# Experts of a routed MoE: a short last tile in 16 instead of 24 matmuls, and a first product with four widths

## The chip, the cores and the metric

The kernel runs on one core of one Trainium2 chip. The metric is the time of one execution in microseconds (us) on the device. TensorE (PE, its weight loads PEld) multiplies, VectorE (DVE), ScalarE (ACT) and GpSimd (POOL) work on tiles of 128 partitions, and SyncE (SP) issues most transfers. Each engine has a queue of its own and runs it in order.

## The reference

Three stages follow each other: a block-recurrent attention over 2 x 768 tokens, a dense layer pair with squared ReLU, and a routed layer with eight experts. The change touches the last one:

```python
for e in range(E):                       # E = 8, N = 1536 tokens, D = 512, F = 1024
    mask = e_idx == e                    # e_idx = argmax(x @ w_gate)
    h = np.maximum(x[mask] @ w1[e], 0.0)
    ye = h @ w2[e]
    out[mask] = gate_w[mask, None] * eom[mask, e, None] * ye
```

On the reference's own inputs the eight experts get 180, 334, 245, 166, 121, 47, 176 and 267 tokens.

## The kernel before

**Numbers in two parts.** Every float32 operand of a large product is split into a high part and a rest (`hh` and `hl`, `xh` and `xl`, `w1h` and `w1l`), both in a reduced format (fp32r). A product is three matmuls: high by high, high by rest, rest by high.

**Tiles of an expert.** The tokens of an expert are numbered and gathered into up to three tiles of 128 rows (`NG` = 3; expert 0 has `NSL` = 2). An expert's 1024 hidden columns are eight blocks f of 128. `emm1(e, f)` is the first product of a block: 12 matmuls whose moving operand is the tokens, so their columns are the tokens. A branch on TensorE takes 384, 256 or 192 columns by the expert's count `cnt[e]`; expert 0 always takes 256. Its result, in one of two PSUM buffers, becomes `hh` on ScalarE (L914) and `hl` on VectorE (L915), so the first product of block f waits for `hl` of block f - 2.

**The second product.** `emm2(e, f, j)` adds block f of tile j into the accumulator `ea[j]`: three matmuls of 128 weight columns and 512 moving columns, `hh` by `w2h`, `hh` by `w2l`, `hl` by `w2h`. Tile 0 is done between the first products, two blocks behind. Tile 1 follows in one piece if the count is over 128 and tile 2 if it is over 256 (branches at L1031 and L1035); otherwise TensorE jumps over them.

**The end of an expert.** `put(e, j)` scales tile j by its gate on ScalarE (L926, output `y`) and GpSimd scatters the rows to the output (L927). The puts are issued for every tile, whether TensorE had it or not; rows without a token are left out by the scatter's index. ScalarE's queue then comes to `hh` of the next expert's block 0.

**Side work.** The weights of the experts are loaded and split between the blocks (L776 on ScalarE, L777 on VectorE). In expert 0 the routing of the last 512 tokens is finished on VectorE between the blocks (`route_count`, `slot_idx`, `route_gate`, `route_gates`), by a table `late` of jobs for each block. The order on each engine is that of the program text.

Of the kernel before, what the change touches and what calls it, by code (L numbers as in the profile page):

```python
# [16 lines left out]
AF = mybir.ActivationFunctionType  # L17
ALU = mybir.AluOpType
# [6 lines left out]
def attn_moe_kernel(ctx, tc, q, k, v, lam, w_in, w_out, w_gate, w_ogate, w1, w2, out):  # L25
    nc = tc.nc
    B, H, S, D = q.shape
    NT, DM = out.shape
    DFF = w_in.shape[1]
    E, _, F2 = w1.shape  # L30
    P = 128
    NCH = S // P
    HP = H // 2
    KC = DM // P
    NF = DFF // P
    NF2 = F2 // P
# [8 lines left out]
    const = ctx.enter_context(tc.tile_pool(name="const", bufs=1))  # L45
# [22 lines left out]
    cnti = const.tile([P, E], I32, name="cnti")  # L68
# [143 lines left out]
    n = 2  # L212
# [24 lines left out]
    for b in range(B):  # L237
        t = cut([P, HP, P])
# [212 lines left out]
    p_ct = prb[:, P + 4 * E:P + 5 * E]  # L451
# [187 lines left out]
    def slot_idx(jsl, es):

        n, m = jsl.stop - jsl.start, es.stop - es.start
        v_ = rp[0].tile([P, n, m], F32, tag="v_", name="v_")
        nc.vector.scalar_tensor_tensor(out=v_, in0=sacc[:, jsl, 1, es], scalar=float(P), in1=sacc[:, jsl, 0, es],
                                       op0=ALU.mult, op1=ALU.add)
        tm = rp[0].tile([P, n, m], F32, tag="tm", name="tm")
        nc.vector.tensor_scalar(out=tm, in0=v_, scalar1=0.0, scalar2=float(BIG), op0=ALU.is_equal, op1=ALU.mult)
        nc.vector.scalar_tensor_tensor(out=sidx[:, jsl, es], in0=v_, scalar=-1.0, in1=tm, op0=ALU.add, op1=ALU.add)
# [175 lines left out]
    ch = NCK - 1  # L823
# [13 lines left out]
    NX = NG * P  # L837
# [8 lines left out]
    pt.append(pe_t.tile([P, KC, P], F32, tag="pt2", name="pt"))  # L846
    ea = [pe_a.tile([P, DM], F32, tag=f"ea{j}", name="ea") for j in range(NG)]
    w2s += [[ep.tile([P, DM], F32R, tag=f"w2{t_}{i}", name=f"w2{t_}") for t_ in "hl"] for i in range(len(w2s), R2)]
    xs_ = [[ep.tile([P, KC, NX], F32R, tag=f"x{t_}{i}", name=f"x{t_}") for t_ in "hl"] for i in range(2)]
    hh = ep.tile([P, NF2, NX], F32R, name="hh")  # L850
    hl = ep.tile([P, NF2, NX], F32R, name="hl")
# [15 lines left out]
    def xpose(e, g):  # L867

        xh, xl = xs_[e % 2]
        src = pt[g]  # L870
        if g < 2:
            cs, ts_ = slice(2 * g, 2 * g + 2), slice(0, NSL * P)
            if e == 0:
                src = xt0[g]
            else:
                for i in range(2):
                    cb = 2 * g + i
                    for j in range(NSL):
                        nc.tensor.transpose(src[:, i, j * P:(j + 1) * P], xg[j][:, cb * P:(cb + 1) * P], ident)  # L879
        else:  # L880
            cs, ts_ = slice(0, KC), slice(NSL * P, NX)
# [7 lines left out]
    def emm1(e, f):  # L889
        s = e * NF2 + f  # L890
        w1h, w1l = w1s[s % R1]
        xh, xl = xs_[e % 2]
        ps = psb[s % 2]

        def go(N):
            mms = [(kk, w_, x_) for kk in range(KC) for w_, x_ in ((w1h, xh), (w1h, xl), (w1l, xh))]
            if s == 0:
                mms.sort(key=lambda m: (m[0] // 2, m[2] is xl))
            for n, (kk, w_, x_) in enumerate(mms):
                nc.tensor.matmul(out=ps[:, 0:N], lhsT=w_[:, kk, :], rhs=x_[:, kk, 0:N], start=n == 0,  # L900
                                 stop=n == 3 * KC - 1)
# [11 lines left out]
        ts_ = slice(0, NSL * P if e == 0 else NX)  # L913
# [4 lines left out]
    def emm2(e, f, j):  # L918
        w2h, w2l = w2s[(e * NF2 + f) % R2]
        js = slice(j * P, (j + 1) * P)  # L920
        for i, (h_, w_) in enumerate(((hh, w2h), (hh, w2l), (hl, w2h))):
            nc.tensor.matmul(out=ea[j], lhsT=h_[:, f, js], rhs=w_, start=f == 0 and i == 0,
                             stop=f == NF2 - 1 and i == 2)

    def put(e, j):
        nc.scalar.activation(out=ys[j], in_=ea[j], func=AF.Copy, scale=gate[:, j, e:e + 1])  # L926
        nc.gpsimd.indirect_dma_start(out=outs[j][:, :], out_offset=bass.IndirectOffsetOnAxis(ap=sidx[:, j, e:e + 1], axis=0),  # L927
                                     in_=ys[j], in_offset=None, bounds_check=NT - 1, oob_is_err=False)

    def load_counts():  # L930
        cnt.extend(nc.values_load_multi_w_load_instructions(
            cnti[0:1, 0:E], engines=(mybir.EngineType.PE,), min_val=0, max_val=NT,
            skip_runtime_bounds_check_because="counts of NT tokens")[1])

    xpose(0, 0)
# [3 lines left out]
    for j in range(NG):  # L939
# [131 lines left out]
```

## Time and profile before

| | us |
|---|---|
| median of 3 runs (572.71 to 574.24) | 573.63 |
| the profiled execution | 573.35 |
| its span, first to last instruction | 571.6 |
| TensorE busy in it | 549.3 |
| VectorE busy in it | 364.4 |
| ScalarE busy in it | 304.0 |

The profiled execution is one run under the hardware profiler; its granted TensorE clock was 0.996 of full speed. The experts take the span from about 355 us on. Busy time of TensorE counts each matmul from its start to its modelled end, and matmuls overlap; how far apart two of them start is the time that one costs.

### The profile page before, as it was taken

Reading aid. Unit: us, or ns where it says so; the run is one execution under the profiler, and the core shown is the slowest. Engines: PE = TensorE matmul, PEld = TensorE weight load, DVE = VectorE, ACT = ScalarE, POOL = GpSimd, SP = SyncE. Lnnn points to the kernel's source line nnn. Section 1 sums busy time; section 2 is a strip of 40 time slices with the busy share of each in tenths; the row PEclk is TensorE's granted clock in tenths of the full one; section 3 lists DMA queues with packets and bytes.
Section 4 is the critical chain, followed back from the end, with each engine's and each line's share of the span. In section 5 each row is a group of like instructions: output and inputs, shape, how many; then the busy total and the mean of one; then the engine's idle time right before and its main releaser. Section 6 shows DMA issues by size and latency. Waiting matters only on the chain. (4 is left out here: it accounts for less than half of the span.)

```text
span 571.6 us, 9445 instructions
## 1 busy us (share of the span) xinstructions
PE 549.3 (96%) x3412; PEld 461.5 (81%) x3412; DVE 364.4 (64%) x731; ACT 304.0 (53%) x577; POOL 151.6 (27%) x153
## 2 busy tenths in 40 slices
PE   6999899999999999999999999899999999999994
PEld 5988788888877877887887888789887988888883
DVE  7679988988455664546676446948264839776510
ACT  4666477776543443435444334536364747885610
POOL 5788100000021232412123241350303142240101
PEclk9999999999999999999999999999999999999998
DMA  9999446468100010000000003999538567840000
GB/s 187 225 252 262 120 147 217 157 216 315 53 0 2 19 37 20 0 1 0 20 18 20 20 0 127 389 256 314 176 119 281 181 213 241 265 153 20 9 24 23
DMA packets 75044, 72.87 MB, mean 127 GB/s; under 512 B 30181, under 2 KB 61029, under 8 KB 74976
## 3 DMA queue, kind: packets, MB, share of 16 engines
q1 hardware_dynamic: 70624, 62.96, 36.5%
q0 software_dynamic: 4064, 8.91, 5.0%
q8 instruction: 42, 0.69, 0.5%
q14 instruction: 26, 0.21, 0.2%
q10 hardware_dynamic: 288, 0.10, 0.1%
HBM read 65.84 MB, written 9.29 MB: 131 GB/s over the span
## 5 line engine op out<-in xcount | busy, mean ns | idle before, releaser
L335 POOL TENSOR_TENSOR wol<-woF,woh 128x512 fp32r<-128x512 f32 x32 | 41.6, 1301 | 228.1 <-ACT woh L334 228.1
L365 DVE TENSOR_TENSOR gl<-g,gh 128x512 fp32r<-128x512 f32 x48 | 52.9, 1103 | 67.8 <-ACT gh L364 67.8
L900 PE MATMUL ph<-xh,xTh 128*128 128x192 f32 (+2 forms) x256 | 77.6, 303 | 6.6 <-issue 2.3
L915 DVE SCALAR_TENSOR_TENSOR hl<-ph,hh 128x384 fp32r<-128x384 f32 (+1 forms) x64 | 34.5, 539 | 68.4 <-ACT hh L914 68.4
L347 PE MATMUL ps<-xTh,wih 128*128 128x512 f32 x192 | 77.6, 404 | 0.0
L463 PE MATMUL acc<-gh,woh 128*128 128x512 f32 x192 | 76.2, 397 | 0.3 <-DVE x1T L475 0.2
L463 PE MATMUL acc<-gl,woh 128*128 128x512 f32 x192 | 75.9, 396 | 0.0
L347 PE MATMUL ps<-xTl,wih 128*128 128x512 f32 x192 | 75.9, 395 | 0.0
L463 PE MATMUL acc<-gh,wol 128*128 128x512 f32 x192 | 75.9, 395 | 0.0
L347 PE MATMUL ps<-xTh,wil 128*128 128x512 f32 x192 | 75.9, 395 | 0.0
L900 PE MATMUL ph<-xh,xTl 128*128 128x192 f32 (+2 forms) x256 | 74.7, 292 | 0.0
L900 PE MATMUL ph<-xl,xTh 128*128 128x192 f32 (+2 forms) x256 | 74.4, 292 | 0.0
L334 ACT CAST woh<-woF 128x512 fp32r<-128x512 f32 x48 | 29.6, 616 | 60.3 <-PE acc L463 60.2
L900 PEld LDWEIGHTS ph<-xh,xTh 128*128 128x128 f32 x256 | 48.7, 190 | 15.2 <-DVE hl L915 7.3
L914 ACT ACTIVATE hh<-ph 128x384 fp32r<-128x384 f32 (+1 forms) x64 | 30.7, 479 | 41.2 <-PE ph L900 38.1
L354 ACT ACTIVATE r<-ps 128x512 f32<-128x512 f32 x48 | 28.6, 595 | 39.1 <-PE ps L347 39.1
L900 PEld LDWEIGHTS ph<-xl,xTh 128*128 128x128 f32 x256 | 48.7, 191 | 0.7
L900 PEld LDWEIGHTS ph<-xh,xTl 128*128 128x128 f32 x256 | 48.8, 191 | 0.0
L859 POOL DMA_INDIRECT xg<-x1d,gidx x21 | 23.5, 1117 | 89.1 <-PE pt L879 66.1
L777 DVE TENSOR_TENSOR xTl<-w1r,xTh 128x512 fp32r<-128x512 f32 x64 | 44.1, 689 | 0.1
L463 PEld LDWEIGHTS acc<-gh,woh 128*128 128x128 f32 x192 | 36.0, 188 | 9.8 <-DVE x1T L475 1.2
L927 POOL DMA_INDIRECT out_dram<-y,sidx x23 | 23.6, 1027 | 76.3 <-ACT y L926 73.9
(182 smaller groups left out, 1163.0 us busy)
## 6 DMA issues: line engine op xcount, KB each, us to landing
w1r<-in_moe_w_dram SPq DMA_DIRECT2D x32, 512.0 KB, 5.9
w2r<-in_moe_w_dram SPq DMA_DIRECT2D x32, 512.0 KB, 6.7
st<-in_moe_w_in_dram SPq DMA_DIRECT2D x16, 512.0 KB, 3.7
st<-in_moe_w_out_dram SPq DMA_DIRECT2D x16, 512.0 KB, 4.3
q<-in_q_dram SPq DMA_DIRECT2D x24, 128.0 KB, 4.4
k<-in_k_dram SPq DMA_DIRECT2D x12, 256.0 KB, 4.7
v<-in_v_dram SPq DMA_DIRECT2D x12, 256.0 KB, 5.1
x1d<-xr SPq DMA_DIRECT2D x12, 256.0 KB, 2.0
```

Source lines behind the costliest of these rows:

```text
L334: nc.scalar.copy(out=hi, in_=src)
L335: eng.tensor_tensor(out=lo, in0=src, in1=hi.bitcast(F32), op=ALU.subtract)
L347: nc.tensor.matmul(out=ps, lhsT=w_[:, kk, :], rhs=x_[:, kk, tk], start=n == 0, stop=n == 3 * KC - 1)
L354: nc.scalar.activation(out=r, in_=ps, func=AF.Relu)
L365: nc.vector.tensor_tensor(out=gl, in0=g, in1=gh.bitcast(F32), op=ALU.subtract)
L463: nc.tensor.matmul(out=acc[ch][cb], lhsT=w_[:, cs], rhs=x_, start=f == 0 and i == 0, stop=f == NF - 1 and i == 2)
L777: eng.tensor_tensor(out=lo, in0=src, in1=hi.bitcast(F32), op=ALU.subtract)
L859: nc.gpsimd.indirect_dma_start(out=out_, out_offset=None, in_=x1d[:, :], in_offset=bass.IndirectOffsetOnAxis(ap=ix, axis=0), bounds_check= ...
L900: nc.tensor.matmul(out=ps[:, 0:N], lhsT=w_[:, kk, :], rhs=x_[:, kk, 0:N], start=n == 0, stop=n == 3 * KC - 1)
L914: nc.scalar.activation(out=hh[:, f, ts_], in_=ps[:, ts_], func=AF.Relu)
L915: nc.vector.scalar_tensor_tensor(out=hl[:, f, ts_], in0=ps[:, ts_], scalar=0.0, in1=hh[:, f, ts_].bitcast(F32), op0=ALU.max, op1=ALU.subtract)
L927: nc.gpsimd.indirect_dma_start(out=outs[j][:, :], out_offset=bass.IndirectOffsetOnAxis(ap=sidx[:, j, e:e + 1], axis=0), in_=ys[j], in_offs ...
```

## The change

**Short last tile.** Where the last tile that an expert uses has at most 64 rows, `hh` and `hl` of these rows stand side by side as one operand `hp` of 64 + 64 columns. One matmul with `w2h` and one with `w2l` then replace three; rows 0 to 63 of `ea[1]` hold the products of the high part, rows 64 to 127 those of the rest. `hp` is filled by a VectorE copy of four blocks at a time (L957), twice per expert. To make the last tile always j = 1, experts with over 256 tokens swap the second and third tile (`COLS`, `to_tiles`). The flag `half`, read by TensorE as `cnt[E + e]`, is set for at most 192 tokens, or over 256 and at most 320.

**Putting it together.** `put(e, 1)` scales the lower half on ScalarE (`yl`, by the gate `gup`, which is zero where the tile isn't halved), adds it to the upper half on VectorE, and does the rest of the tile on ScalarE.

**First product.** Its columns are 384 for over 320 tokens, 320 for 257 to 320, 256 for 193 to 256, and 192 below; the columns now start at the tile's place in the new order.

```diff
+    def to_tiles(t_, eng):
+        d_ = rp[0].tile([P, E], F32, tag="d_", name="d_")
+        eng.tensor_tensor(out=d_, in0=t_[:, 2], in1=t_[:, 1], op=ALU.subtract)
+        eng.tensor_tensor(out=d_, in0=d_, in1=big, op=ALU.mult)
+        eng.tensor_tensor(out=t_[:, 2], in0=t_[:, 1], in1=big, op=ALU.mult)
+        eng.tensor_tensor(out=t_[:, 1], in0=t_[:, 1], in1=d_, op=ALU.add)
+
+    def route_half():
+        nc.vector.scalar_tensor_tensor(out=half, in0=cntf, scalar=320.0, in1=big, op0=ALU.is_le, op1=ALU.mult)
+        nc.vector.scalar_tensor_tensor(out=half, in0=cntf, scalar=192.0, in1=half, op0=ALU.is_le, op1=ALU.add)
+        nc.vector.tensor_copy(out=cnti[:, E:2 * E], in_=half)
...
@@ route_gates
+        to_tiles(gate, nc.vector)
+        nc.scalar.copy(out=gup[P // 2:P], in_=gate[0:P // 2, 1])
+        nc.vector.tensor_tensor(out=gup[P // 2:P], in0=gup[P // 2:P], in1=half[P // 2:P], op=ALU.mult)
...
@@ route_count
-        nc.vector.tensor_copy(out=cnti, in_=p_ct)
+        nc.vector.tensor_copy(out=cntf, in_=p_ct)
+        nc.vector.tensor_copy(out=cnti[:, 0:E], in_=p_ct)
+        nc.vector.tensor_tensor(out=big, in0=cntf, in1=c256, op=ALU.is_gt)
...
@@ emm1
+        def arms(lo, cut):
+            with tc.If(cnt[e] > cut) as c1:
+                go(lo, NX)
+            with c1.Else():
+                go(lo, NX - P // 2)
+
         if e == 0:
-            go(NSL * P)
+            go(P, NX)
         else:
             with tc.If(cnt[e] > NSL * P) as c0:
-                go(NX)
+                arms(0, 320)
             with c0.Else():
-                with tc.If(cnt[e] > 192) as c1:
-                    go(NSL * P)
-                with c1.Else():
-                    go(192)
+                arms(P, 192)
...
+        if f % 4 == 3:
+            fs, rs = slice(f - 3, f + 1), slice(NSL * P, NSL * P + P // 2)
+            nc.vector.tensor_copy(out=hp[:, fs].rearrange("p f w t -> p w f t"), in_=h2[:, :, fs, rs])
...
@@ emm2
+        if halves:
+            h_ = hp[:, f].rearrange("p w t -> p (w t)")
+            mms = [(h_, w2h), (h_, w2l)]
+        else:
+            mms = [(hh[:, f, js], w2h), (hh[:, f, js], w2l), (hl[:, f, js], w2h)]
...
@@ put
+        if j == 1:
+            lo, hi = slice(0, P // 2), slice(P // 2, P)
+            nc.scalar.activation(out=yl[lo], in_=ea[j][hi], func=AF.Copy, scale=gup[hi, e:e + 1])
+            nc.vector.scalar_tensor_tensor(out=ys[j][lo], in0=ea[j][lo], scalar=gate[lo, j, e:e + 1], in1=yl[lo],
+                                           op0=ALU.mult, op1=ALU.add)
+            nc.scalar.activation(out=ys[j][hi], in_=ea[j][hi], func=AF.Copy, scale=gate[hi, j, e:e + 1])
...
@@ the expert loop
         with tc.If(cnt[e] > P):
-            for f in range(NF2):
-                emm2(e, f, 1)
+            with tc.If(cnt[E + e] > 0) as c2:
+                for f in range(NF2):
+                    emm2(e, f, 1, True)
+            with c2.Else():
+                for f in range(NF2):
+                    emm2(e, f, 1)
```

The built program of TensorE grows from 4,650 to 5,490 rows, since both arms stand in it. Three places show how the order on the engines moves.

VectorE in expert 0, between the splits of block 1 and `hl` of block 2 (`pt` is the routing's PSUM buffer, `sacc` the slots, `gidx` the gather's index), before:

```order
L666 CAST cnti<-pt 128x8
L668 TENSOR_TENSOR over<-pt,caps 128x8
L669 TENSOR_REDUCE overi<-over 128x1
L634 TENSOR_TENSOR sacc<-sacc,pt 128x3x16
L643 SCALAR_TENSOR_TENSOR v__3811<-sacc 128x24
L646 TENSOR_SCALAR tm<-v__3811 128x24
L647 SCALAR_TENSOR_TENSOR sidx<-v__3811,tm 128x24
L637 TENSOR_SCALAR gidx<-sidx 128x24
L915 SCALAR_TENSOR_TENSOR hl<-ph,hh 128x256
```

The same place of the changed kernel, from the first new row (the row of `cnti` between `cntf` and `big` included) to the same `hl`:

```order
L692 COPY cntf<-pt 128x8
L693 CAST cnti<-pt 128x8
L694 TENSOR_TENSOR big<-cntf,c_96 128x8
...
L664 SCALAR_TENSOR_TENSOR v__3821<-sacc 128x24
L649 TENSOR_TENSOR d__3823<-v__3821 128x8
L650 TENSOR_TENSOR d__3823<-d__3823,big 128x8
L651 TENSOR_TENSOR v__3821<-v__3821,big 128x8
L652 TENSOR_TENSOR v__3821<-v__3821,d__3823 128x8
L669 TENSOR_SCALAR tm<-v__3821 128x24
L670 SCALAR_TENSOR_TENSOR sidx<-v__3821,tm 128x24
L644 TENSOR_SCALAR gidx<-sidx 128x24
L953 SCALAR_TENSOR_TENSOR h_3712<-ph,h_3712 128x256
```

Six rows stand ahead of `hl` (now the second half of the tile `h_`) that weren't there. The copy into `hp` (L957) and three rows of `route_half` (L656 to L658) come between the following blocks in the same way.

ScalarE at an expert's end, from the last transposed tile of the next expert (`xh`) to the next expert's first `hh`, before:

```order
L884 CAST xh<-pt 128x4x128
L1031 UNCONDITIONAL_BRANCH
L926 ACTIVATE y<-ea,gate 128x512 x2
L906 UNCONDITIONAL_BRANCH x2
L926 ACTIVATE y<-ea,gate 128x512
L914 ACTIVATE hh<-ph 128x384
```

And in the changed kernel, where the first row below is `y` of tile 0:

```order
L979 ACTIVATE y<-ea,gate 128x512
L1084 UNCONDITIONAL_BRANCH
L974 ACTIVATE yl<-ea,gup 64x512
L947 UNCONDITIONAL_BRANCH x2
L977 ACTIVATE y<-ea,gate 64x512
L979 ACTIVATE y<-ea,gate 128x512
L952 ACTIVATE h_3712<-ph 128x384
```

The one `y` of tile 1 became `yl` and a `y` of 64 rows, and the second of them waits for VectorE's multiply-add of `ea` and `yl` (L975).

TensorE at tile 1 of expert 0 in the changed kernel, the branch and the first of its 16 matmuls; the 24 of the other arm stand behind the jump:

```order
L1084 COMPARE_AND_BRANCH
L1085 COMPARE_AND_BRANCH
L968 MATMUL ea<-xTh,hp 128x512
L968 MATMUL ea<-xTl,hp 128x512
...
L1085 UNCONDITIONAL_BRANCH
L968 MATMUL ea<-xTh,h_3712 128x512
L968 MATMUL ea<-xTl,h_3712 128x512
```

Before, one branch (L1031) and 24 matmuls stood there; now a second branch chooses between two lists.

## Rows read from the trace of the kernel before

**Rows 1.** Page, part 1: busy us, share, instructions.

```profile
PE 549.3 (96%) x3412; PEld 461.5 (81%) x3412; DVE 364.4 (64%) x731; ACT 304.0 (53%) x577; POOL 151.6 (27%) x153
```

**Rows 2.** Busy by stretch, experts 0 and 4; length, busy, granted clock, DMA share, GB/s.

```profile
355.10:382.60 27.50, 25.59 (x181) 22.18 (x182) 20.75 (x72) 12.78 (x28) 12.15 (x11) 1.00 1.05 320
...
466.30:486.00 19.70, 18.56 (x133) 16.25 (x132) 15.58 (x27) 14.76 (x29) 4.97 (x5) 1.00 0.61 202
```

**Rows 3.** Timeline of TensorE, tile 1 of expert 0: start, length, what, idle before.

```profile
378.59 0.39 PE L922 MATMUL ea<-xTh,hh 128*128 128x512 f32 x1
...
382.44 0.39 PE L922 MATMUL ea<-xTh,hl 128*128 128x512 f32 x1
```

**Rows 4.** Timeline of TensorE: first products of 384 and of 256 columns.

```profile
382.67 0.33 PE L900 MATMUL ph<-xh,xTh 128*128 128x384 f32 x1
...
388.93 0.39 PE L922 MATMUL ea<-w2h,hh 128*128 128x512 f32 x1
389.16 0.40 PE L922 MATMUL ea<-w2l,hh 128*128 128x512 f32 x1
...
418.64 0.28 PE L900 MATMUL ph<-xh,xTh 128*128 128x256 f32 x1
...
419.85 0.28 PE L900 MATMUL ph<-xl,xTh 128*128 128x256 f32 x1
```

**Rows 5.** Timeline of TensorE in expert 0: the two longest waits.

```profile
366.50 0.39 PE L900 MATMUL ph<-xh,xTh 128*128 128x256 f32 x1 [0.78 <-DVE hl L915]
...
369.77 0.39 PE L900 MATMUL ph<-xh,xTh 128*128 128x256 f32 x1 [0.88 <-DVE hl L915]
```

**Rows 6.** Timeline of VectorE in expert 0: small operations, and a gap.

```profile
362.12 0.18 DVE L643 SCALAR_TENSOR_TENSOR v__3811<-sacc 128x24 f32<-128x24 f32 x1
362.34 0.18 DVE L646 TENSOR_SCALAR tm<-v__3811 128x24 f32<-128x24 f32 x1
...
369.15 0.16 DVE L586 TENSOR_SCALAR tg<-tok 128x4 int32<-128x4 f32 x1
369.22 0.17 DVE L588 COPY tg<-gt 128x4 f32<-128x4 f32 x1
...
374.85 0.42 DVE L915 SCALAR_TENSOR_TENSOR hl<-ph,hh 128x256 fp32r<-128x256 f32 x1 [0.29 <-ACT hh L914]
```

**Rows 7.** VectorE's copies of 512 columns: two in the timeline.

```profile
9.44 0.39 DVE L233 COPY ca<-ca 64x512 f32<-64x512 f32 x1
10.93 1.17 DVE L233 COPY ca<-ca 64x512 f32<-64x512 f32 x1
```

**Rows 8.** Timelines of ScalarE, VectorE and TensorE from expert 4 to 5.

```profile
486.13 1.84 ACT L926 ACTIVATE y<-ea,gate 128x512 f32<-128x512 f32 x3 [0.81 <-PE ea L922]
488.44 0.49 ACT L914 ACTIVATE hh<-ph 128x384 fp32r<-128x384 f32 x1 [0.47 <-PE ph L900]
...
488.96 0.56 DVE L915 SCALAR_TENSOR_TENSOR hl<-ph,hh 128x384 fp32r<-128x384 f32 x1 [2.92 <-ACT hh L914]
...
491.89 0.19 PEld L900 LDWEIGHTS ph<-xh,xTh 128*128 128x128 f32 x1 [0.45 <-DVE hl L915]
```

**Rows 9.** Timelines of ScalarE and TensorE from expert 2 to 3.

```profile
441.54 1.26 ACT L926 ACTIVATE y<-ea,gate 128x512 f32<-128x512 f32 x2 [4.77 <-PE ea L922]
444.26 0.49 ACT L914 ACTIVATE hh<-ph 128x384 fp32r<-128x384 f32 x1 [1.46 <-PE ph L900]
...
442.64 0.36 PE L900 MATMUL ph<-xh,xTh 128*128 128x192 f32 x1 [1.14 <-issue]
```

**Rows 10.** One line's branches (min/median/max ns, who waited), and the page's instruction queue.

```profile
L906 PEldq COMPARE_BRANCH  x72: 73/208/1647, 378.9 to 547.5; - x72
...
who waited for it (us, times):
...
q8 instruction: 42, 0.69, 0.5%
```

**Rows 11.** Timeline of ScalarE at the end: the last `y`.

```profile
564.02 0.69 ACT L926 ACTIVATE y<-ea,gate 128x512 f32<-128x512 f32 x1 [4.75 <-PE ea L922]
```

More of the change, by code (lines that the diff above doesn't have):

```diff
@@ L67, in attn_moe_kernel @@
     nc.gpsimd.memset(wg, 0.0)
-    cnti = const.tile([P, E], I32, name="cnti")
+    cnti = const.tile([P, 2 * E], I32, name="cnti")
     over = const.tile([P, E], F32, name="over")
@@ L80, in attn_moe_kernel @@
     gate = const.tile([P, NG, E], F32, name="gate")
+    COLS = [slice(P, 2 * P), slice(2 * P, 3 * P), slice(0, P)]
+    c256 = const.tile([P, E], F32, name="c256")
+    nc.gpsimd.memset(c256, float(NSL * P))
+    nc.gpsimd.memset(c256[:, 0:1], float(BIG))
     pp1 = const.tile([P, 1], F32, name="pp1")
@@ L635, in slot_fin, with slot_idx @@
         if ch == NCK - 1 and lo == 0:
-            slot_idx(jsl, slice(0, E))
+            slot_idx(jsl, slice(0, E), True)
             nc.vector.tensor_scalar(out=gidx[:, jsl], in0=sidx[:, jsl], scalar1=NT - 1, scalar2=None, op0=ALU.min)
-    def slot_idx(jsl, es):
+    def to_tiles(t_, eng):
[8 more added lines that the diff above has]
+        nc.vector.tensor_copy(out=cnti[:, E:2 * E], in_=half)
+    def slot_idx(jsl, es, last=False):
         n, m = jsl.stop - jsl.start, es.stop - es.start
@@ L644, in slot_idx @@
                                        op0=ALU.mult, op1=ALU.add)
+        if last:
+            to_tiles(v_, nc.vector)
         tm = rp[0].tile([P, n, m], F32, tag="tm", name="tm")
@@ L848, in attn_moe_kernel @@
     w2s += [[ep.tile([P, DM], F32R, tag=f"w2{t_}{i}", name=f"w2{t_}") for t_ in "hl"] for i in range(len(w2s), R2)]
+    cntf = ep.tile([P, E], F32, name="cntf")
+    big = ep.tile([P, E], F32, name="big")
+    half = ep.tile([P, E], F32, name="half")
+    gup = ep.tile([P, E], F32, name="gup")
+    yl = ep.tile([P, DM], F32, name="yl")
     xs_ = [[ep.tile([P, KC, NX], F32R, tag=f"x{t_}{i}", name=f"x{t_}") for t_ in "hl"] for i in range(2)]
-    hh = ep.tile([P, NF2, NX], F32R, name="hh")
-    hl = ep.tile([P, NF2, NX], F32R, name="hl")
+    h2 = ep.tile([P, 2, NF2, NX], F32R, name="h2")
+    hh, hl = h2[:, 0], h2[:, 1]
+    hp = ep.tile([P, NF2, 2, P // 2], F32R, name="hp")
     xg = [ep.tile([P, DM], F32, tag=f"xg{j}", name="xg") for j in range(NG)]
@@ L880, in xpose @@
         else:
-            cs, ts_ = slice(0, KC), slice(NSL * P, NX)
+            cs, ts_ = slice(0, KC), COLS[2]
             for cb in range(KC):
@@ L899, in go @@
             for n, (kk, w_, x_) in enumerate(mms):
-                nc.tensor.matmul(out=ps[:, 0:N], lhsT=w_[:, kk, :], rhs=x_[:, kk, 0:N], start=n == 0,
+                nc.tensor.matmul(out=ps[:, lo:hi], lhsT=w_[:, kk, :], rhs=x_[:, kk, lo:hi], start=n == 0,
                                  stop=n == 3 * KC - 1)
+        def arms(lo, cut):
[3 more added lines that the diff above has]
+                go(lo, NX - P // 2)
         if e == 0:
-            go(NSL * P)
+            go(P, NX)
         else:
             with tc.If(cnt[e] > NSL * P) as c0:
-                go(NX)
+                arms(0, 320)
             with c0.Else():
-                with tc.If(cnt[e] > 192) as c1:
-                    go(NSL * P)
-                with c1.Else():
-                    go(192)
-        ts_ = slice(0, NSL * P if e == 0 else NX)
+                arms(P, 192)
+        ts_ = slice(P if e == 0 else 0, NX)
         nc.scalar.activation(out=hh[:, f, ts_], in_=ps[:, ts_], func=AF.Relu)
@@ L916, in emm1, with emm2 @@
                                        op0=ALU.max, op1=ALU.subtract)
-    def emm2(e, f, j):
+        if f % 4 == 3:
+            fs, rs = slice(f - 3, f + 1), slice(NSL * P, NSL * P + P // 2)
+            nc.vector.tensor_copy(out=hp[:, fs].rearrange("p f w t -> p w f t"), in_=h2[:, :, fs, rs])
+    def emm2(e, f, j, halves=False):
         w2h, w2l = w2s[(e * NF2 + f) % R2]
[L920 to L923, printed above, removed]
-    def put(e, j):
-        nc.scalar.activation(out=ys[j], in_=ea[j], func=AF.Copy, scale=gate[:, j, e:e + 1])
+        js = COLS[j]
+        if halves:
[3 more added lines that the diff above has]
+            mms = [(hh[:, f, js], w2h), (hh[:, f, js], w2l), (hl[:, f, js], w2h)]
+        for i, (h_, w_) in enumerate(mms):
+            nc.tensor.matmul(out=ea[j], lhsT=h_, rhs=w_, start=f == 0 and i == 0, stop=f == NF2 - 1 and i == len(mms) - 1)
+    def put(e, j):
+        if j == 1:
[4 more added lines that the diff above has]
+            nc.scalar.activation(out=ys[j][hi], in_=ea[j][hi], func=AF.Copy, scale=gate[hi, j, e:e + 1])
+        else:
+            nc.scalar.activation(out=ys[j], in_=ea[j], func=AF.Copy, scale=gate[:, j, e:e + 1])
         nc.gpsimd.indirect_dma_start(out=outs[j][:, :], out_offset=bass.IndirectOffsetOnAxis(ap=sidx[:, j, e:e + 1], axis=0),
@@ L931, in load_counts @@
         cnt.extend(nc.values_load_multi_w_load_instructions(
-            cnti[0:1, 0:E], engines=(mybir.EngineType.PE,), min_val=0, max_val=NT,
+            cnti[0:1, 0:2 * E], engines=(mybir.EngineType.PE,), min_val=0, max_val=NT,
             skip_runtime_bounds_check_because="counts of NT tokens")[1])
@@ L945, in attn_moe_kernel @@
             2: [lambda: route_gate(ch), lambda: route_gate1(ch)],
-            3: [lambda: route_gate2(ch)],
+            3: [lambda: route_gate2(ch), route_half],
             6: [lambda: slot_mm(ch, list(range(NG)), 2), lambda: slot_fin(ch, list(range(NG)), 2),
```

4 lines of the change are left out of this document (2 added, 2 removed).

## The prediction

> **What bounds the kernel now.** I read the page first: TensorE is busy 549.3 of 571.6 us [rows 1], so a change in its own work should show. Then the busy time by stage: expert 0's stretch, 355.10 to 382.60, has 25.59 of 27.50 us of TensorE and 20.75 of VectorE, with a matmul clock of 1.00; a later expert's, 466.30 to 486.00, has 18.56 of 19.70 against 15.58 [rows 2]. So the experts are TensorE's time plus short waits, and the waits decide what the added work on VectorE and ScalarE costs. Two kinds were read in the timeline. In expert 0 the first product stands still before 366.50 and 369.77, both times for `hl` of VectorE [rows 5], and VectorE runs through those stretches with hardly a gap. At the start of the experts that follow short ones, TensorE drains on its own branches and then meets ScalarE's queue [rows 8].
>
> **What is removed from TensorE.** By the token counts, experts 0, 3, 6 and 7 (180, 166, 176 and 267 tokens) have a last tile of at most 64 rows and take 16 in place of 24 matmuls in that tile; 1 and 2 (334, 245) keep 24, 4 and 5 have no second tile. A 512-column matmul is issued every (382.44 - 378.59)/17 = 0.2265 us [rows 3]. The form is the same (128 weight columns, 512 moving), so 4 experts x 8 x 0.2265 = **7.25 us**. The fourth arm changes only expert 7: 96 matmuls go from 384 to 320 columns. 384 columns take (388.93 - 382.67)/36 = 0.174 us and 256 take (419.85 - 418.64)/10 = 0.121 [rows 4]; no 320 was run, and half way is 0.1475, 0.0265 less each: **2.54 us**. Its bounds are 0 (as slow as 384) and 5.1 (as quick as 256); issue follows columns from 256 to 512, so I take the middle. Together 9.8 us.
>
> **Expert 0's VectorE.** All that is added there before `hl` of block 4 delays TensorE in full. Dependent small operations start 0.22 us apart (362.12, 362.34), independent ones 0.07 (369.15, 369.22) [rows 6]. The two of `route_count` (one waiting for the other): 0.2. The four of `to_tiles` (three in a chain): 0.7. The three of `route_half`: 0.5. The `hp` copy of 512 elements: a copy of 64x512 took 0.39 us beside nothing, another of the same shape 1.17 with GpSimd at work [rows 7]; I take 0.5, because its source is in SBUF and GpSimd issues only gathers there. Sum **1.9 us**, bounds 1.2 (the shorter pitches and 0.39) and 2.8 (1.17 and every small one at 0.22 or more). [...] The further gate work (four small operations, a ScalarE copy, a multiply) comes in block 6 where `hl` of block 7 has a gap of 0.29 us ahead of it [rows 6] and is needed only for the last matmuls of tile 0, several microseconds of TensorE later; I put it at nothing, and at up to 1 if that cover is gone.
>
> **The handoff at an expert's end.** `put(e,1)` becomes ScalarE `yl`, then VectorE's multiply-add, then ScalarE `y`, which waits for VectorE with everything behind it on ScalarE's queue: `y` of tile 2 and then `hh` of the next expert's block 0, for which `hl`, and through it the first product of block 2, wait. This is issued whether the expert has a second tile or not. At the end of expert 4 the three copies `y` are back to back from 486.13, 0.575 us apart (1.84 us for three, the last 0.69), and `hh` follows at 488.44, as soon as its product is done [rows 8]. After: `yl` at 486.70 to 487.39, 0.03 us to the other engine (`hh` ends 488.93, `hl` starts 488.96 [rows 8]), 0.69 of multiply-add to 488.11, `y` at 488.14, the next `y` at 488.72, `hh` at 489.29 rather than 488.44: 0.85 us late. Block 2 waits already for `hl` (0.45 us of idle before 491.89 [rows 8]), so all of it arrives. The ends of experts 4 and 5 are alike: **1.7 us**, bounds 1.0 (a multiply-add of 64 rows at 0.39) and 2.6 (1.3 each). At the ends of experts 2 and 3 only two copies stand in a row: 441.54 plus 0.69, 0.72, 0.03, 0.58 and 0.58 is 444.14, and `hh` starts at 444.26 [rows 9]. It just fits; I put 0.1 at each of the two, 0 to 0.4. At experts 0, 1 and 6 one copy stands in the way, or the chain runs beside the last tile's matmuls, and there is room.
>
> **What else moves.** `hp` copies of experts 1 to 7, two of some 0.5 us each per expert, lie in VectorE's idle time (15.58 of 19.70 [rows 2]); if that cover were gone they would cost up to 7 us. The counts are loaded for 16 numbers rather than 8 in TensorE's queue, ahead of the work that uses them. Expert 7's arm has one more branch per block; taken branches take 0.2 us at the median [rows 10] and run ahead of the matmuls except at the drained start, 0.2 us once. The end still follows TensorE: the last `y` starts 564.02 after 4.75 us idle for the last matmul [rows 11].
>
> **Sum.** -9.8 + 1.9 + 1.7 + 0.2 + 0.2 = -5.8 us. The profiled execution took 573.35 us (span 571.6 and 1.75 around it), 0.28 under the median of 573.63; on the median it is **567.8 us**.
>
> **Rivals.** *The added work costs less*: multiply-add and copy at 0.39, the cover holds everywhere. Expert 0 is 1.2, the handoffs 1.0, nothing else: -7.6, **566.0 us**. For it: half the partitions; against: elsewhere the time follows columns. *It costs more*: expert 0 at 2.8, handoffs at 1.3 for five ends rather than 0.85 for two (6.5), the branch 0.2: -0.3, **573.3 us**; with the copy alone at 1.17 and three ends at 1.0 it is -9.8 + 2.6 + 3.0 + 0.2 = -4.0, 569.6. Against: rows 9 show room at two ends. *The instruction stream*, the other side: each second and third tile now holds two arms of which one is jumped over, eight such jumps (one an expert), and the program is longer. The longest branch of L906 held the queue 1.65 us [rows 10]; if every new jump held TensorE so long, 8 x 1.65 = 13.2 us against 5.8 gained is **581 us**. It decides from 5.8/8 = 0.73 us a jump, and makes the time over 0.3% worse from 7.5/8 = 0.94. Against it: no engine waited for that longest branch (the answer's line on who waited is empty), the median is 0.21, and the matmuls around it keep their pitch, 388.93 and 389.16 [rows 4]. The instruction queue moved 42 packets in 0.5% of 16 engines' time [rows 10], 0.005 x 16 x 571.6 / 42 = 1.1 us each, and as TensorE's program grows from 4,650 to 5,490 rows it would be some 7 more: 7.7 us if none were hidden, which alone eats the gain. [...] *The change does less than it says*: were expert 7 or another not to take its short arm, 1.8 us each less; two of them out gives 571.4.
>
> **How the numbers follow.** The forecast (566.4 to 569.6) has 0.68, cheaper 0.12, dearer 0.10, instruction stream 0.06, fewer arms 0.04. A measurement of this kernel tells about 0.3%, 1.7 us, from no change: faster under 571.9, slower over 575.3. Faster: 0.68 + 0.12 + some 0.04 of the dearer + 0.02 of the fewer arms = 0.86; same: the rest of these two, 0.08; slower: 0.06. The range takes in the cheaper case with 320 columns a little quicker, and most of the dearer one: 565.0 to 571.0.
>
> **What would show it.** 128-row tiles of `hp` in 64 matmuls at 0.2265 us; 96 matmuls of 320 columns near 0.1475; expert 0's waits before blocks 5 and 6 about 1.9 us longer in sum; `hh` of experts 5 and 6 some 0.85 us behind its product; the drained starts of experts 3 to 7 unchanged (1.14 us before 442.64 [rows 9]). Wrong would be: new idle time of TensorE with "issue" or a branch as its end in the middle of an expert, the short arms at another pitch, or waits for VectorE in experts 1 to 7.

## The result: slower, and the profile after

The changed kernel takes 577.99 us (576.89 to 581.29, 5 runs); the ratio to the kernel before is 1.0082, interval [1.0063, 1.0101]. It is 4.4 us slower, and the forecast of 567.8 us was wrong. Each ratio in this document compares a kernel with runs of the kernel before that were made beside it, and leaves out runs over 1.5% above the fastest of their kernel.

TensorE does have less to do, and the instruction queue q8 moved six packets more than before [rows 1, 10]. Its packets, 0.79 MB / 48 = 16 KB each, are called instruction pages here; their number goes with the length of TensorE's program, from 28 at 2,763 rows in the shortest kernel below to 48 at 5,490. From the page of the changed kernel:

```profile
PE 541.6 (94%) x3380; PEld 452.6 (79%) x3380; DVE 378.6 (66%) x769; ACT 310.1 (54%) x586; POOL 153.6 (27%) x155
...
q8 instruction: 48, 0.79, 0.6%
```

The halves run as meant. Groups of lines of the changed kernel: 26 + 26 + 6 + 6 = 64 matmuls with `hp`, the copy into `hp` at 466 ns and the multiply-add at 742. (`xTh` and `xTl` in these names are weight buffers that lie where tiles of these names lay before.)

```profile
L968 PE MATMUL ea<-xTh,hp 128*128 128x512 f32 x26 | 10.4, 400 | 0.0
L968 PE MATMUL ea<-xTl,hp 128*128 128x512 f32 x26 | 10.2, 394 | 0.0
L968 PE MATMUL ea<-w2h,hp 128*128 128x512 f32 x6 | 2.4, 394 | 0.0
L968 PE MATMUL ea<-w2l,hp 128*128 128x512 f32 x6 | 2.4, 392 | 0.0
...
L957 DVE CAST hp<-h 128x512 fp32r<-128x512 f32 x16 | 7.5, 466 | 0.6
L975 DVE SCALAR_TENSOR_TENSOR y<-ea,gate,yl 64x512 f32<-64x512 f32 x8 | 5.9, 742 | 30.7 <-ACT yl L974 30.7
```

Its timeline on TensorE shows the fourth width in expert 7, 320 columns every (541.77 - 540.31)/10 = 0.146 us:

```profile
540.31 0.31 PE L935 MATMUL ph<-xh,xTh 128*128 128x320 f32 x1
...
541.77 0.31 PE L935 MATMUL ph<-xl,xTh 128*128 128x320 f32 x1
```

and the waits, those of expert 0 (the answer to [rows 5]) and three others that have no counterpart before:

```profile
369.63 0.39 PE L935 MATMUL ph<-xh,xTh 128*128 128x256 f32 x1 [0.74 <-DVE h L953]
372.75 0.39 PE L935 MATMUL ph<-xh,xTh 128*128 128x256 f32 x1 [0.73 <-DVE h L953]
376.96 0.39 PE L935 MATMUL ph<-xh,xTh 128*128 128x256 f32 x1 [1.82 <-DVE h L953]
...
396.13 0.50 PE L968 MATMUL ea<-w2h,h 128*128 128x512 f32 x1 [1.28 <-ACT xTh L804]
...
477.99 0.36 PE L935 MATMUL ph<-xh,xTh 128*128 128x192 f32 x1 [1.25 <-DVE xTl L805]
...
498.98 0.36 PE L935 MATMUL ph<-xh,xTh 128*128 128x192 f32 x1 [1.93 <-DVE xTl L805]
```

The releasers named in the last three are splits of weights that ended nearby, not what was waited for: they ended 0.23 to 0.54 us before the matmul, where `h` of VectorE ended 0.05 us before the matmul at 376.96. The branch ahead of them says more (below).

To see where the time went, every profiled execution is cut at the same places, read from TensorE's timeline: the attention up to its last matmul, the second stage up to the matmul of `route_count`, each expert up to the first product of the next, expert 7 up to the last matmul. All stretches are us; the kernels are those of the experiments.

```
              atten-  stage
              tion    two     e0    e1    e2    e3    e4    e5    e6    e7
before        69.68  288.94  24.05 34.55 25.43 25.01 19.17 19.17 24.46 33.49
after         75.03  289.00  24.32 36.45 25.58 23.43 20.31 20.99 24.20 29.25
b_plus64      72.83  289.05  24.04 34.58 25.35 25.02 19.18 19.17 24.46 33.49
b_plus128     71.91  289.88  24.04 34.96 25.42 25.00 19.19 19.16 24.44 33.49
b_vshift      71.28  288.93  24.04 34.55 25.46 24.95 19.17 19.17 24.54 33.47
b_qk512       69.14  288.91  24.03 34.63 25.43 25.00 19.17 19.17 24.44 33.48
a_oldaddr     70.82  288.91  25.67 34.82 25.56 23.39 20.13 22.75 24.18 29.28
a_three_old   71.07  288.91  24.41 35.00 25.33 23.40 19.41 20.67 23.72 31.79
b_four        70.53  288.92  24.14 38.33 25.25 24.89 19.21 23.80 24.71 30.75
b_four_s64    72.73  288.92  24.04 35.55 25.26 25.03 19.47 21.63 24.69 30.75
v1_relief     69.45  288.91  24.56 35.16 25.48 23.36 19.31 21.75 23.35 31.79
v_hand        69.45  288.92  24.50 34.72 25.48 23.39 19.33 21.09 23.35 31.80
v_e7          70.28  288.91  24.49 34.79 25.49 23.31 19.31 20.20 23.57 29.20
v_fixed       70.99  288.91  24.47 34.73 24.33 22.94 19.21 19.91 23.65 29.30
v_best        69.19  288.92  24.40 34.72 25.47 23.38 19.31 21.47 23.55 29.20
```

The surprise stands in the first column: the attention, which the diff does not touch, is 5.35 us longer, more than the whole loss. The experts together are 0.8 us shorter instead of 5.8: experts 1, 4 and 5 lose 1.9, 1.1 and 1.8 us, where 0, 0.1 and 0.85 were forecast.

### The profile page after: what moved, and what is told of

The parts are those of the page before. It is cut to its first block, busy times and chain, and to the rows that moved or that the text cites. A ratio compares the mean times of both kernels' runs of the same rounds, so it can differ in the third digit from the quotient of the medians.

```text
span 576.3 us, 9428 instructions
## 1 busy us (share of the span) xinstructions
PE 541.6 (94%) x3380; PEld 452.6 (79%) x3380; DVE 378.6 (66%) x769; ACT 310.1 (54%) x586; POOL 153.6 (27%) x155
## 5 line engine op out<-in xcount | busy, mean ns | idle before, releaser
L935 PE MATMUL ph<-xh,xTh 128*128 128x192 f32 (+3 forms) x256 | 76.3, 299 | 13.2 <-DVE h L953 4.3
L935 PE MATMUL ph<-xh,xTl 128*128 128x192 f32 (+3 forms) x256 | 73.7, 288 | 0.0
L935 PE MATMUL ph<-xl,xTh 128*128 128x192 f32 (+3 forms) x256 | 73.5, 289 | 0.0
L968 PE MATMUL ea<-xTh,h 128*128 128x512 f32 x152 | 56.7, 402 | 0.0
L953 DVE SCALAR_TENSOR_TENSOR h<-ph,h 128x384 fp32r<-128x384 f32 (+1 forms) x64 | 34.4, 537 | 30.8 <-ACT h L952 30.5
L361 ACT ACTIVATE r<-ps 128x512 f32<-128x512 f32 x48 | 28.5, 595 | 39.2 <-PE ps L354 39.2
L952 ACT ACTIVATE h<-ph 128x384 fp32r<-128x384 f32 (+1 forms) x64 | 30.7, 480 | 35.1 <-PE ph L935 33.6
L894 POOL DMA_INDIRECT xg<-x1d,gidx x21 | 25.2, 1200 | 90.8 <-PE pt L914 66.4
```

What stands on the lines that cost most here:

```text
L361: nc.scalar.activation(out=r, in_=ps, func=AF.Relu)
L894: nc.gpsimd.indirect_dma_start(out=out_, out_offset=None, in_=x1d[:, :], in_offset=bass.IndirectOffsetOnAxis(ap=ix, axis=0), bounds_check= ...
L935: nc.tensor.matmul(out=ps[:, lo:hi], lhsT=w_[:, kk, :], rhs=x_[:, kk, lo:hi], start=n == 0, stop=n == 3 * KC - 1)
L968: nc.tensor.matmul(out=ea[j], lhsT=h_, rhs=w_, start=f == 0 and i == 0, stop=f == NF2 - 1 and i == len(mms) - 1)
```

## The experiments

Two theories. **Place**: among the constants `cnti` grows and `c256` is new, 64 bytes in each partition together; they push the tiles allocated behind them 64 bytes up, and loads into such places are slower; against it, that the longer program slows them. The buffers that q and k are loaded into don't move: they are allocated from the other end (`side="right"`). **Pages**: TensorE waits for instruction pages of its longer program; against it, that the jumps over a tile's second list, the handoff, or VectorE and ScalarE make these waits.

**b_plus64**, the place alone:

```diff
+    pad = const.tile([P, 16], F32, name="pad")
+    nc.gpsimd.memset(pad, 0.0)
     pp1 = const.tile([P, 1], F32, name="pp1")
```

> The kernel before with 64 bytes more per partition in its constants and nothing else; every tile behind them moves up by 64 bytes, as in the change. If the place of the tiles slows the attention's loads, the attention ends some 5.5 us later, as in the changed kernel (63.03 against 57.50 us), and the time is near 579 us. If the loads are slower for another reason (the longer program, or where inputs lie), the time stays at 573.6 and the attention ends near 57.5.

577.69 us, ratio 1.0070 [1.0047, 1.0092]; the attention ends 3.15 us later and nothing else changes. The place alone makes the kernel before as slow as the change. (The 57.50 and 63.03 us of the expectation are an earlier mark, the start of one and the same matmul `po<-qd,ca`.) TensorE's longest waits for a transfer in the first 76 us, before and in the change (us in total, times, longest):

```profile
PEld psk L252 <- DMA k<-in_k_dram: 0.9, 1, 0.9
```
```profile
PE psq L257 <- DMA q<-in_q_dram: 4.8, 5, 1.4
```

The loads of q come late although q's buffers did not move; they share the queue q1 with the loads that did, but no run separates this. The attention's own length differs by 1.6 us between executions of kernels with the old places (69.45 to 71.07 in the table; in the two longest, a_three_old and v_fixed, the granted clock was 0.51 from 14.5 to 17.9 us). The 2.2 us between 3.15 and 5.35 are little more than that, and whether they are a second effect stays open.

**a_oldaddr**, the change with the places of before:

```diff
-    cnti = const.tile([P, 2 * E], I32, name="cnti")
+    spare = const.tile([P, E], I32, name="spare")
...
-    c256 = const.tile([P, E], F32, name="c256")
...
+    cnti = ep.tile([P, 2 * E], I32, name="cnti")
+    c256 = ep.tile([P, E], F32, name="c256")
...
```

> The changed kernel with its new constants moved to the experts' pool, so that all tiles of the first two stages lie where they lay before. If the place matters: the attention ends near 57.5, and the time is 578.0 - 5.5 = 572.5 us. If the longer program is what slows the loads: 578 us.

575.8 us (573.13 to 578.04), ratio 1.0031 [1.0011, 1.0051] in place of 1.0082. The attention is at 70.82; the longer program is not what slowed it. By the runs the places cost 0.0051 of the time in the change, 2.9 us. The time is over the expected 572.5. In the profiled execution the attention is 1.1 us longer than before, and in the experts it is the clock, not the page waits, that differs from the change's profile. The waits are 1.10 us in expert 4 and 2.09 in expert 5, near the change's 1.25 and 1.93. But soon after expert 0's wait of 1.84 us for `hl` and after expert 5's, the granted clock fell to half for 3.4 us (the seventh number):

```profile
372.90:376.30 3.40, 3.40 (x15) 3.13 (x15) 2.79 (x6) 0.70 (x2) 2.75 (x3) 0.50 1.04 395
495.70:499.10 3.40, 3.40 (x15) 3.11 (x15) 3.07 (x6) 1.70 (x4) 0.00 (x0) 0.51 0.86 291
```

TensorE is busy throughout, so each costs some 1.7 us (3.4 x 0.50, an estimate): expert 0 takes 25.67 us in place of the change's 24.32, expert 5 22.75 in place of 20.99.

**b_vshift**, only v's buffers 64 bytes higher, and **b_plus128**, all that b_plus64 moved, 128 bytes higher:

```diff
+    vpad = sa.enter_context(tc.tile_pool(name="vpad", bufs=1))
+    pad = vpad.tile([P, 16], F32, name="pad")
+    nc.gpsimd.memset(pad, 0.0)
     ldv = sa.enter_context(tc.tile_pool(name="ldv", bufs=4))
```
```diff
+    pad = const.tile([P, 32], F32, name="pad")
+    nc.gpsimd.memset(pad, 0.0)
     pp1 = const.tile([P, 1], F32, name="pp1")
```

> The kernel before, in which only the four buffers that v is loaded into lie 64 bytes higher. If the place of the loads' destination is what costs in the attention, its end is some 3 us later as with everything moved (72.83 against 69.68 us), and the time is near 577 us. If the place of other tiles (the staged weights, the states) matters, nothing changes: 574 us.

> The kernel before with all tiles behind the constants 128 bytes higher, not 64. If only places that are no multiple of 128 bytes cost, the time is that of before, 574 us; if every place off the old one does, it is near 577.5 us as with 64 bytes.

b_vshift: 575.6 us, ratio 1.0028 [1.0013, 1.0043], attention +1.6 us. That lies between its two expectations. So the destination of a load matters by itself; v is 0.4 to 0.5 of it (0.28 of 0.70% by the runs, 1.6 of 3.15 us by the profiles). b_plus128: 578.22 us, ratio 1.0067 [1.0050, 1.0085]; 64 or 128 bytes off, the cost is about the same.

**b_qk512**, the other way round: q's and k's buffers, 480 bytes off a multiple of 512 before, are put onto one (v's were on one).

```diff
+    qpad = sqk.enter_context(tc.tile_pool(name="qpad", bufs=1, side="right"))
+    pad = qpad.tile([P, 120], F32, name="pad")
+    nc.gpsimd.memset(pad, 0.0)
     ldqk = sqk.enter_context(tc.tile_pool(name="ldqk", bufs=4, side="right"))
```

> The kernel before, in which only the buffers of q and k lie 480 bytes lower, on a multiple of 512 bytes, as those of v do. If a destination off such a multiple makes loads slower, q's and k's packets get quicker and the attention ends 1.5 to 4 us sooner than 69.7: about 571 us. If only v or the staged weights matter, the time is unchanged, 573.5 us.

572.8 us, ratio 0.9983 [0.9970, 0.9996]: a little faster, by less than expected (the attention ends 0.5 us sooner). The transfers themselves show it plainly. The row of the load queue (packets, MB, share of 16 engines) in the first 60 us of before, the change, b_plus64, b_plus128, b_vshift and b_qk512, in this order:

```profile
q1 hardware_dynamic: 34175, 13.64, 101.5%
```
```profile
q1 hardware_dynamic: 32168, 12.25, 107.2%
```
```profile
q1 hardware_dynamic: 32930, 12.77, 108.1%
```
```profile
q1 hardware_dynamic: 33758, 13.03, 106.1%
```
```profile
q1 hardware_dynamic: 34005, 13.17, 108.3%
```
```profile
q1 hardware_dynamic: 34176, 13.64, 89.5%
```

Share x 60 us x 16 engines / packets gives 28.5 ns a packet before (q and k off), 32.0 in the change, 31.5 and 30.2 with v's and all other moved tiles 64 and 128 higher, 30.6 with v's alone, and 25.1 with q, k and v all on a multiple of 512. It repeats: the eight other kernels with the old places have 28.1 to 29.2, and v_best, with q and k as here, 24.9. The reader should see that the change moved 1.4 MB less in the same 60 us with engines that were busier. Why such a place costs is in no row here. The places run off a multiple of 512 are 64 and 128 bytes above one for v, and 480 for q and k; whether a multiple of some smaller size would do as well was not run.

**b_four**, the long program without the halves: only the fourth width.

```diff
             with tc.If(cnt[e] > NSL * P) as c0:
-                go(NX)
+                with tc.If(cnt[e] > 320) as c2:
+                    go(NX)
+                with c2.Else():
+                    go(320)
```

> The kernel before with only the fourth width of the first product added: a program of 5,434 rows, no short last tile. Expert 7's columns give 2.5 us. If the longer program brings late pages, there are again stalls of 1 to 2 us in several experts, 4 to 6 us in sum, and the time is 575 to 577 us. If the late pages come from the jumps over the second list of a tile, there are none here and the time is 571.1 us.

Ten runs spread from 571.6 to 582.0 us (median 578.38, ratio 1.0034 [1.0000, 1.0068]). The quickest is near the 571.1 expected without page waits. In the profiled execution, one of 579.95 us, experts 1 and 5 take 3.8 and 4.6 us more than before, with no halves, no handoff and no second list to jump over. Its timeline on TensorE, and the busy time by stretch (the seventh number is the granted clock):

```profile
392.26 0.80 PE L925 MATMUL ea<-w2l,hh 128*128 128x512 f32 x1 [2.02 <-issue]
...
494.86 0.53 PE L900 MATMUL ph<-xl,xTh 128*128 128x192 f32 x1 [1.89 <-issue]
```
```profile
385.00:392.00 7.00, 5.25 (x30) 4.87 (x29) 5.59 (x10) 5.59 (x11) 0.76 (x1) 1.00 0.94 271
392.00:396.00 4.00, 3.74 (x12) 3.55 (x13) 0.75 (x2) 0.00 (x0) 0.00 (x0) 0.57 1.04 387
...
494.90:500.30 5.40, 5.40 (x24) 5.36 (x25) 3.13 (x6) 2.24 (x6) 0.56 (x1) 0.50 0.91 297
```

"issue" is a wait for nothing that the profile shows. After each the granted clock fell to half (0.50), for 3.4 us from 392.2 and for 6.8 us from 494.6, which costs about as much again: expert 5 waits 1.9 us and loses 4.6. The clock goes with the spread, too: the mean granted clock of the quickest run is 0.995 and of the slowest 0.984. If TensorE is busy throughout, that is (0.995 - 0.984) x 582 = 6.4 of the 10.4 us between them, an estimate.

**b_four_s64**, the same with 64 tiny matmuls at its start, whose results nothing uses and which put the experts' code further back in TensorE's program:

```diff
     warm_pe(9)
+    for _ in range(64):
+        nc.tensor.matmul(out=pw_[:, 0, 0:1], lhsT=ones, rhs=ones[:, 0:1], start=True, stop=True)
```

> [...] If the stalls in experts 1 and 5 (3.8 and 4.6 us more than before) are late pages, they move to other places or change by over 1 us. If they belong to the branches of these blocks, they stay in the same two experts at the same size. [...]

577.88 us (573.51 to 579.94), ratio 1.0059 [1.0036, 1.0083], with the attention 2.2 us longer (the granted clock was 0.50 from 8.5 to 18.7 us). The waits are in the same two experts but at other places of them: in expert 1 5.1 us after its start in place of 8.7, in expert 5 6.7 in place of 3.6.

```profile
390.81 0.41 PE L902 MATMUL ph<-xh,xTh 128*128 128x384 f32 x1 [0.77 <-ACT hh L919]
...
497.69 0.50 PE L927 MATMUL ea<-xTl,hh 128*128 128x512 f32 x1 [2.08 <-issue]
```

After the wait of 2.08 us the clock stayed at 1.00, and expert 5 loses 2.5 us instead of 4.6. The new places speak for pages, but b_four itself varies by 10 us from run to run, so their sizes in two profiles prove nothing.

**a_three_old**, a_oldaddr without the fourth width (43 pages instead of 48):

```diff
             with tc.If(cnt[e] > NSL * P) as c0:
-                arms(0, 320)
+                go(0, NX)
```

> As the last kernel, but the first product has its three widths back (384, 256, 192), so TensorE's program is 4,706 rows rather than 5,490; the short last tile stays. If the stalls inside experts 1, 4, 5 and 6 (5.9 us together) are instruction pages fetched too late because the program is longer, they shrink to those of before: against the kernel with the old places -5.9, +2.5 for the columns of expert 7, and +1.5 for handoffs that the stalls now cover: about 570.5 us. If the jumps over the second list of a tile cause them, they stay and the time is 572.5 + 2.5 = 575 us.

572.74 us (572.03 to 574.3), ratio 0.9970 [0.9957, 0.9984]. Against the change, experts 1 to 6 give back 1.45 + 0.25 + 0.03 + 0.90 + 0.32 + 0.48 = 3.4 us and expert 7 loses the 2.5 of its columns. The jumps over the second list are all still there, so they are not the price. 570.5 was expected; what is left in experts 5 and 6 is the handoff. ScalarE, VectorE and TensorE from expert 4 to 5 in this kernel (the place of [rows 8]):

```profile
487.56 0.68 ACT L976 ACTIVATE yl<-ea,gup 64x512 f32<-64x512 f32 x1
489.05 0.68 ACT L979 ACTIVATE y<-ea,gate 64x512 f32<-64x512 f32 x1 [0.81 <-DVE y L977]
489.76 0.69 ACT L981 ACTIVATE y<-ea,gate 128x512 f32<-128x512 f32 x1
490.35 0.48 ACT L954 ACTIVATE h<-ph 128x384 fp32r<-128x384 f32 x1
```
```profile
488.27 0.74 DVE L977 SCALAR_TENSOR_TENSOR y<-ea,gate,yl 64x512 f32<-64x512 f32 x1 [1.24 <-ACT yl L976]
...
490.86 0.56 DVE L955 SCALAR_TENSOR_TENSOR h<-ph,h 128x384 fp32r<-128x384 f32 x1 [1.84 <-ACT h L954]
```
```profile
491.47 0.36 PE L937 MATMUL ph<-xh,xTh 128*128 128x192 f32 x1 [1.02 <-DVE h L955]
```

ScalarE stands still for 0.81 us, `hh` starts at 490.35, and the third block waits 1.02 us for its `hl`.

**v1_relief** and **v_hand** put tile 2's `y` ahead of the half copy in experts 1 to 6 (`put_lo` does `yl` and the multiply-add, and gives back the rest); v1_relief also moves expert 0's copy into `hp` and `route_half` behind the block that TensorE waits for, and moves one operation of `route_count` into `route_half`.

```diff
+        if 0 < e < E - 1:
+            hi_ = put_lo(e)
+            put(e, 2)
+            hi_()
...
-        if f % 4 == 3:
+        if f == 7 or f == (5 if e == 0 else 3):
...
-            3: [lambda: route_gate2(ch), route_half],
+            3: [lambda: route_gate2(ch)],
+            4: [route_half],
```

> The kernel with three widths and the old places, and beside these: the next tile's copy stands ahead of the half copy that waits for VectorE (experts 1 to 6), and in expert 0 the copy into hp and the flag for the halves come after the block for which TensorE waits. If the 1.0 to 1.2 us that experts 5 and 6 wait before their third block is the handoff, these waits fall to 0.2 each and expert 0's stretch is 1 us shorter: 572.7 - 2 - 1 = 569.7 us. If these waits are late instruction pages, they stay, and the time is 571.7 us.

> The kernel with three widths and the old places, and with the next tile's copy ahead of the half copy that waits for VectorE; expert 0 as in the change. If the handoff was the wait of 1.0 to 1.2 us in experts 5 and 6: -1.4 us against that kernel's 572.7, 571.3 us, and no wait in expert 0 before its second tile (1.0 us in the kernel with the work of expert 0 put later). If late pages rule whatever is changed, 572 to 573 us.

v1_relief: 571.51 us, ratio 0.9946 [0.9927, 0.9964]; v_hand: 572.69, ratio 0.9980 [0.9968, 0.9992]. In v_hand's timeline the wait of expert 5's third block falls from 1.02 to 0.44 us:

```profile
489.15 0.35 PE L937 MATMUL ph<-xh,xTh 128*128 128x192 f32 x1 [0.44 <-DVE h L955]
```

so it was the handoff. The time of v_hand did not move (0.9980 beside 0.9970 of a_three_old, and in the 572 to 573 us that its expectation gave to late pages), and that of v1_relief moved less than expected: a page wait came back in expert 5 (21.09 us in v_hand, 21.75 in v1_relief), now behind the third block. In expert 0 the relief did not help: 24.56 us against 24.50, since the work put later was late for tile 1:

```profile
370.38 0.38 PE L937 MATMUL ph<-xh,xTh 128*128 128x256 f32 x1 [1.05 <-DVE h L955]
...
377.64 0.50 PE L971 MATMUL ea<-xTh,h 128*128 128x512 f32 x1 [0.83 <-ACT h L954]
```

The first is 0.77 us shorter than the change's 1.82, the second is new. The timed runs nevertheless put v1_relief ahead of v_hand, on another chip and with intervals that don't touch, while its profile has the experts 1.1 us longer; page waits that differ from run to run could do that, which no run shows.

**v_e7**, v_hand with the fourth width only in expert 7's code, so that it runs the matmuls of the change in 43 pages:

```diff
             with tc.If(cnt[e] > NSL * P) as c0:
-                go(0, NX)
+                if e == E - 1:
+                    arms(0, 320)
+                else:
+                    go(0, NX)
```

> The last kernel with the fourth width in the code of expert 7 alone (4,818 rows of TensorE's program rather than 5,490). On these inputs it runs the same matmuls as the change. If the length of the program was the price of the fourth width, its gain of 2.4 us now arrives: 568.9 us. If the fourth width's branches in expert 7 cost, 571 us or more.

570.15 us (568.92 to 570.55), ratio 0.9941 [0.9922, 0.9960]. The 2.4 us of the fourth width arrive as soon as experts 1 to 6 don't carry its code. The experts take 4.95 us less than before, near the forecast's 5.8.

**v_fixed**: each expert's code holds only what it runs on these inputs, so it computes the reference for these counts alone.

```diff
-        if e == 0:
-            go(P, NX)
-        else:
...
+        go(*[(P, NX), (0, NX), (P, NX), (P, 320), (P, 320), (P, 320), (P, 320), (0, 320)][e])
```

> The kernel with the reordered handoff, in which each expert's code holds only the matmuls that it runs on these inputs (no branches on the counts; 2,763 rows), so it holds for these inputs alone. It runs the same matmuls as the change. If the stalls of 1 to 2 us and the 0.7 to 1.3 us at drained starts belong to instruction pages and branches, none is left: experts 205.3 - 9.7 + 2.1 + 0.6 - 4.8 = 193.5 us, the time 562 us. If the stalls belong to VectorE and ScalarE, they stay, and the time is 566 to 568 us.

568.77 us, ratio 0.9923 [0.9897, 0.9949], 28 pages. No wait for a page and no drained start is left, but the time is 7 us over the first expectation and just over the second: the drained starts had covered ScalarE's copies. Now the third block waits for `hl`, 0.72 us each in experts 3 and 4 and 1.43 each in 5 and 6, 4.3 us together (the attention is 1.3 us longer than before, too). In expert 5:

```profile
489.83 0.36 PE L937 MATMUL ph<-xh,xTh 128*128 128x192 f32 x1 [1.43 <-DVE h L949]
```

**v_best**, v_e7 with q's and k's buffers as in b_qk512:

> The version with the reordered handoff and the fourth width in expert 7 alone (570.15 us), with the q and k buffers on a multiple of 512 bytes. If that place helps: 567 to 568.5 us. If not: 570 us.

569.11 us (568.32 to 570.24), ratio 0.9912 [0.9885, 0.9938], within a microsecond of the expected range. It beats both kernels, though its interval overlaps v_e7's; expert 5 has a page wait again (1.31 us before 494.82, a stretch of 21.47 us), so some of this still hangs on where such waits fall. As in v_e7, the choice of the expert with the fourth width fits these counts.

## Why the prediction was wrong

**TensorE's work: right.** 64 matmuls with `hp`; 7.25 us forecast, and expert 3 is 1.58 shorter in place of 1.81, expert 7 4.24 in place of 1.81 + 2.54. The halved matmuls are a little slower than assumed: expert 0's 16 start (388.13 - 384.55)/15 = 0.239 us apart, not 0.2265. A matmul of 320 columns takes 0.146 us where 0.1475 was interpolated.

**Expert 0's VectorE: right.** 24.32 = 24.05 - 1.81 + 2.08 us; 1.9 was forecast. Most of it is one wait, the 1.82 us before 376.96, and not the two of [rows 5] made longer. The `hp` copy, priced at 0.5 between 0.39 and 1.17 [rows 7], took 0.43 there. "The further gate work" cost nothing that can be separated.

**The handoff: the mechanism right, the size too small.** The forecast had `hh` 0.85 us late at expert 5; in a_three_old it is 490.35 - 489.12 (end of its product) = 1.23. Three terms were too short: `yl` starts 487.56 - 486.84 = 0.72 after the `y` before it, not 0.575, the multiply-add is 0.74, not 0.69, and the first ScalarE copy after the wait holds the next for 0.71, not 0.575. The stretches of experts 5 and 6 grow by 1.50 and 1.07 us where 0.85 each was forecast; "it just fits" at experts 2 and 3 held (0.2 each).

**The instruction stream: named, priced and weighed wrongly.** It was the rival with a chance of 0.06. The step that failed is "no engine waited for that longest branch" as evidence against a price. The line on who waited is just as empty in the change's answer (min/median/max ns), though TensorE stood still behind the longest of these branches:

```profile
L939 PEldq COMPARE_BRANCH  x80: 65/208/4028, 384.8 to 554.1; - x80
...
who waited for it (us, times):
```

The 1.65 us before [rows 10] were free because matmuls queued ahead of that branch lasted to its end. In the change the three branches ahead of the waits were held 4.03, 3.07 and 3.75 us, and the matmuls ahead of them ended 1.2 to 1.9 us too early. The one ahead of the wait before 477.99 (that line from 474.6 to 478 us), and the instruction queue in the transfers of 475 to 478:

```profile
L939 PEldq COMPARE_BRANCH  x1: 3065/3065/3065, 474.9 to 474.9; - x1
```
```profile
q8 instruction: 1, 0.02, 2.0%
```

It was held 3.07 us while one page came; the last matmul ahead of it ended at 476.74. In each of the change's three holds one page's transfer lies, with its end at 394.71, 476.54 and 497.57, and TensorE goes on 1.42, 1.45 and 1.41 us after it. A hold as long is free where the matmuls last: in a_three_old a branch was held 3.06 us from 390.4, in expert 1, and TensorE did not stop there.

```profile
L949 PEldq COMPARE_BRANCH  x72: 73/207/3062, 380.7 to 548.9; - x72
```

The count of jumps (eight) was wrong as a measure: a_three_old has them all and loses 3.4 us less. What the waits follow is the length of the code (43 pages against 48). Which branch is held for a page, and why, is not shown. Nor does each such wait stand at a branch: b_four's of 2.02 us before 392.26 stands ahead of the second of a block's three matmuls, where the code has no branch.

**The attention: in no case of the forecast.** "What else moves" listed instructions, not places: the tiles of `const` were taken as free. 5.35 us of the profiled execution's 4.6 are here. By the runs it is less: 2.9 us in the change (a_oldaddr against it), 4.0 in b_plus64.

The terms as measured: -9.7 of matmuls, +2.1 in expert 0, +3.4 in experts 1 to 6 of a_three_old (handoff for the most part), +3.4 of pages, +5.4 of the attention: +4.6 us. They are differences of single executions, so the sum comes out by construction. What stays open: how much of the attention's loss belongs to the staged weights, which were not moved alone, where page waits fall, which differs between executions, and after which waits the clock falls.

## What to carry to other kernels

Before pricing instructions, compare where the tiles lie: 64 bytes of constants at the bottom cost 4.0 us here, where the change without them, with the shorter code and the reordered handoff (v_e7), gained 3.4, and showed up 300 us away from the edit. Arms that are not taken count: 48 pages with the fourth width in seven experts, 43 with it in one, 28 with the taken arms alone. Give an arm only to the code that needs it, and where a branch is held for a page, look at how long the work queued ahead of it lasts, not at a list of who waited. A copy that waits for another engine belongs behind the copies that don't (v_hand: the wait of expert 5's third block fell from 1.02 to 0.44 us).

## What the runs showed of the hardware that was not expected

- Loads into buffers 64 or 128 bytes off a multiple of 512 took 30 to 32 ns a packet (q and k were off by 480 as well), with q, k and v on one 25, with q and k alone off 28 to 29.
- After waits of 1.89 and 2.02 us in b_four, 1.84 and 2.09 in a_oldaddr, the granted clock was 0.50 for 3.4 to 6.8 us; after 1.82 and 1.93 us in the change, 1.84 in a_three_old and 2.08 in b_four_s64 it stayed at 1.00. The length of the wait alone does not tell which.
- The runs of b_four, with page waits of 2.02 and 1.89 us in its profile, span 10 us, with mean granted clocks of 0.984 to 0.996; those of a_three_old span 2.3, with 0.990 to 0.996.
